# Attention, dense layers and top-2 experts in one kernel: the attention's opening by head, its transfers in a written order, and fillers while rows are gathered

## The chip, the cores and the metric

The kernel runs on one core of a Trainium2 chip. The core has TensorE (PE in the rows: matmuls, and PEld for its weight loads), VectorE (DVE), ScalarE (ACT), GpSimd (POOL) and SyncE (SP, which here only issues transfers). The engines run on their own and wait for each other by semaphores. The metric is the time of one execution on the device in microseconds (us); smaller is better. The profile is one execution, taken by the hardware profiler.

## What is computed

Three layers in a row, all in float32: attention with rotary positions over 2 batches x 8 heads x 576 places x 64 dimensions; a dense layer 512 -> 2048 -> 512 with a leaky maximum on 1152 tokens; and a layer of 8 experts (512 -> 1024 -> 512), of which each token takes the two with the highest noisy score.

```python
q_rot, k_rot = (rotate(q), rotate(k))              # x1*cos - x2*sin | x1*sin + x2*cos
scores = scale * np.matmul(q_rot, k_rot.transpose(0, 1, 3, 2))
scores = scores - np.max(scores, axis=-1, keepdims=True)
attn = np.exp(scores)
attn = attn / (np.sum(attn, axis=-1, keepdims=True) + 1e-09)
x = np.matmul(attn, v)                             # then to tokens x 512
h = x @ w_in
x = np.maximum(0.01 * h, h) @ w_out
# experts: the two highest of x @ w_gate + log1p(exp(x @ w_noise)) * noise, then
h = np.maximum(x[mask] @ w1[e], 0.0)
out[mask] += top2_w[mask, k, None] * (h @ w2[e])
```

## The kernel before

Numbers are kept to nearly float32 by splitting an operand into a high part (what PE's fast float32 form keeps) and a low part (the rest), and adding products of both.

**Attention** goes over eight pairs of heads. For a pair: q and k are loaded (`load_qk`), rotated by four elementwise operations for each of the two (`rope`: times cos, two halves times sin, the sum), and turned on PE (`turn`, L329 for one head of pair 0, L331 for both heads at once). ScalarE copies the high part out of PSUM (`turn_high`, L340), VectorE makes the low part (`turn_low`, L356), and small transfers on the chip copy high parts to other partitions (`turn_copy`, TQ<-TQ and TK<-TK; for the first k ScalarE does it, L346). A first set of products gives only each row's maximum (`max_scores` on PE, L377; `max_reduce` on VectorE, L384; five or nine tiles). The maxima are turned to a row (`max_turn`, L394 and L398) and put beside q by ScalarE (head 0 of pair 0, L403) or by a transfer (`max_put`, TQ<-mr), so that the second set of products (`scores`, L427) comes out less its maximum. ScalarE takes the exponential (L433), PE multiplies by v (`values`, L446, which also sums the rows), and the sums go by four small transfers, a reciprocal on VectorE and a product on GpSimd into x.

The order of all this is written out by hand: the string `ORDER` has a letter for each step (M, D: product and maximum; S, W: scores and exponential; V: values; O, P: a rotation on VectorE, on GpSimd; Q, K: turning q, k; a, b, e: the copies; l: loading q, k; F and the signs ! # $ % & *: loading and converting the first six weight tiles of the dense layer; o: a filler, `busy`, a matmul on zeros that keeps PE at work). Every engine but SP runs its steps in the order of the letters. On SP the order of the transfers was left to a scheduler. Three PSUM buffers (the digit behind a letter) take M, S, Q, K and R in turn, one takes V.

In the opening, pair 0 is loaded with both heads in one transfer, and its eight rotations of head 0 stand on VectorE, those of head 1 on GpSimd, both as soon as the data are there. All later rotations are GpSimd's. The conversion of the first weight tiles (L199 to L212) starts in pair 0.

**Dense layer** (L586, L595): 16 slices of weights, converted as it goes. **Experts**: the routing is worked out, an expert's rows are gathered from memory by GpSimd's indirect transfers (`gather`, L890: three of at most 128 rows), turned on PE (`turn_x`, L730) and multiplied (L586, L999). Fillers stand on PE before and between these.

Of the kernel before, what the change touches and what calls it, by code (L numbers as in the profile page):

```python
# [82 lines left out]
def fused_kernel(ctx, tc, q, k, v, w_in, w_out, w_gate, w_noise, noise, w1, w2, consts, out):  # L83
# [149 lines left out]
    ET = mybir.EngineType  # L233
    order = ExitStack()
    order.enter_context(tc.manual_schedule(engines={ET.PE, ET.Activation, ET.DVE, ET.Pool}))
    raw, TQ, TK, VF, VT = [], [], [], [], []
    for i in range(NSET):
        if i < 2:
# [63 lines left out]
    def rope(pr, n, eng, i, a0=0, a1=2):  # L302
        x = raw[pr % 2][n]
        if (pr, n) not in roped:
            roped[pr, n] = [a2.tile([128, KT, 2, D], F32, name=m) for m in ("rope_" + n, "rope_t")]
        hs = slice(a0, a1)
        r, t = (y[:, :, hs] for y in roped[pr, n])
        rv, tv = (y.rearrange("p j h d -> p h j d") for y in (r, t))
        if i == 0:
            eng.tensor_tensor(rv, x[:, hs], cosb[:, hs], op=OP.mult)  # L310
        elif i < 3:
            o, z = (0, 32) if i == 1 else (32, 0)
            eng.tensor_tensor(tv[..., o:o + 32], x[:, hs, :, z:z + 32], sinb[:, hs, :, o:o + 32], op=OP.mult)
# [193 lines left out]
    ORDER = (
"cucluyuluyulxffyflfxzywzxwIzxwzvwvOPvOlvOPlvOPwOoooooooooooooooooQ0POwOhPQ1wOjK2aPhPwijPabnlPooooK0lM1iM2lDPbn"
"oM1lPDM0lPDM2lZDoM1ZPDZM0ZDZM2ZPDM1ZlPDM0lDPR2FDFQ1mFS2PhlR0hjamjPWeK0eS2PiaS1inPVbWnbWVlP!lS2!#lS0$PWM1VWPDM2"
"!M0PDM1VDS2PlDM0Wl%S1M2PD&FVWDPR0US1*PM2mtV#WDePS0l$M1WS2lVDPW%Q0P!#FM1hK2PDVhajiaR1PjVbmineS1&PeS0nWVb*PWl$M2"  # L510
"PUwS1M0wWVDtP!DM1tS2DwVWPw%M0lS1#PTlDPVsW$lM2FS0%lVDWl#R1BM0$mS2BVeWDM1U%S2M0DWtVDNS2VWXQ1M0YhK2DVhajPiaR0jVbm"
"ineS0PeS1nWPbVWPM2wUS0DM1wWVDPtM2tS0DwVPWwPM1lS2TDsPVlWM0lS1DlVWBBR2M0mS1DeVWM2US0DM1WtVNDS2VXWYQ0M1hK2DPVhaji"
"aR1jVbmPineS1PeS0nWbVPWM2wUS1DPM0wWVDtM2tPS1DwVPWwM0PS2TDsVWM1S0DVBWBR2M1mS0DeVWM2US1DM0WNtVDS2VXWYQ1M0hK2DPVh"
"ajiaR0jVPbmineS0PeS1nWPbVWM2wUS0PDM1wWVDtM2PtS0DwVPWwPM1S2TDsVWM0S1DVBWBR2M0mS1DeVWM2US0DM1WNtVDS2VXWYQ0M1hK2D"
"VhajiaR1jVbmineS1eS0nWbVWM2wUS1DM0wWVDtM2tS1DwVWwM0S2TDsVWM1S0DVBWBR2M1mS0DeVWM2US1DM0WtNVDS2VXWQ1YM0hK2DVhaji"
"aR0jVbmineS0&eS1nWbV*WM2wUS0DM1wWVDt&M2tS0&*wVWDw!M1*S0TDsVW#$M2S1DVWB%R0BM2mS1D&eVW*M0US2DM1WtVDNS0VWXM2S1DVY"
"WR0VmeS2eVWS1US0WtVtWVS2TVsWS1VWS0BVWBS2US1WtVWVNVVXVYUtt")
# [637 lines left out]
```

## Time and profile before

| | |
|---|---|
| time, median of 3 runs | 671.38 us (670.01 to 676.26) |
| the profiled execution's own time, and its span | 673.01 us, 670.9 us |
| PE busy | 639.8 us (95% of the span) |
| DVE, ACT, POOL busy | 398.3, 317.0, 170.3 us |
| granted PE clock, mean over the span | 0.990 of full |
| attention, PE's first filler to its last product by v | 1.3 to 182 us |
| dense layer | 182 to about 396 us |
| routing and first gather | about 396 to 412 us |
| experts | 412 us to the end |

A row of a timeline has the start in us from the span's beginning, the time from the first to the last instruction of the row, engine, line, operation, out<-in, shapes, and how many; in brackets the time in which the engine stood idle before it, and what it waited for. Matmuls overlap each other, so the pace of PE is read from the distance of two starts. The granted clock 1.00 is 2.4 GHz, 0.50 is 1.2 GHz.

### The profile page before, as it was taken

The page shows a single profiled execution, that of the slowest core. Times are in us where ns is not written, and L with a number is a line of the kernel's source. Part 1 is how long each engine was busy: PE and PEld are TensorE (multiplying, and loading weights), DVE is VectorE, ACT ScalarE, POOL GpSimd, SP SyncE. Part 2 cuts the span into 40 slices and gives each one's busy share as a digit, 9 for nine tenths or more (in the row PEclk, how much of TensorE's full clock was granted, in tenths as well). Part 3 has the DMA queues.
Part 4 walks back from the last instruction along what each step waited for, and adds up shares of the span by engine and source line. Part 5 has one row for each costly group of instructions (what it writes and reads, how often), then busy time and mean ns, then how long its engine had stood idle before and what let it go on. Part 6 is the DMA issues. An engine that isn't in the chain of part 4 may idle for free. (4 is left out here: it accounts for less than half of the span.)

```text
span 670.9 us, 10384 instructions
## 1 busy us (share of the span) xinstructions
PE 639.8 (95%) x3655; PEld 551.3 (82%) x3659; DVE 398.3 (59%) x830; ACT 317.0 (47%) x643; POOL 170.3 (25%) x179
## 2 busy tenths in 40 slices
PE   7698999999999999999999998999999999999993
PEld 3487788888878888889799975888888888888882
DVE  8788555556069988863237664565665656575611
ACT  4454556665444644432235441545454545454511
POOL 9973777111111000000000001132305050504102
PEclk9999999999999999999999998999999999999998
DMA  6657433325039443310164442557667575848423
GB/s 175 196 159 225 117 74 81 73 67 198 27 111 331 149 129 126 126 48 0 63 236 126 126 112 54 166 132 198 151 210 170 160 205 158 204 147 203 103 28 41
DMA packets 88958, 90.70 MB, mean 135 GB/s; under 512 B 21443, under 2 KB 66694, under 8 KB 88902
## 3 DMA queue, kind: packets, MB, share of 16 engines
q1 hardware_dynamic: 84006, 79.11, 40.0%
q0 software_dynamic: 4608, 10.49, 7.8%
q8 instruction: 30, 0.49, 0.3%
q10 hardware_dynamic: 288, 0.39, 0.2%
q14 instruction: 26, 0.21, 0.1%
HBM read 69.95 MB, written 14.19 MB: 125 GB/s over the span
## 5 line engine op out<-in xcount | busy, mean ns | idle before, releaser
L218 DVE TENSOR_TENSOR wl<-raw,wh 128x512 fp32r<-128x512 f32 x108 | 72.5, 688 | 49.7 <-ACT wh L216 48.4
L1016 POOL DMA_INDIRECT out<-y_row,idx x24 | 41.2, 1718 | 177.0 <-ACT y_row L1008 172.6
L216 ACT ACTIVATE wh<-raw 128x512 fp32r<-128x512 f32 x108 | 66.5, 629 | 34.1 <-DMA raw<-in_moe_w 33.4
L384 DVE TENSOR_REDUCE maxes<-pM 128x1 fp32r<-128x576 f32 (+1 forms) x73 | 54.2, 754 | 43.2 <-PE pM L377 42.5
L890 POOL DMA_INDIRECT got<-x_rows,idx x24 | 23.6, 985 | 216.5 <-DVE gate L842 199.8
L999 PE MATMUL bank<-wh,g_x 128*128 128x512 f32 x216 | 78.4, 403 | 0.1
L446 PE MATMUL pO<-p,VF 128*128 128x288 f32 x256 | 72.7, 413 | 0.0
L433 ACT ACTIVATE p<-pS 128x576 f32<-128x576 f32 (+1 forms) x73 | 46.4, 649 | 53.2 <-PE pS L427 51.6
L586 PE MATMUL bank<-xe_h,wh 128*128 128x320 f32 x216 | 67.8, 314 | 0.0
L586 PE MATMUL bank<-xe_h,wl 128*128 128x320 f32 x216 | 67.7, 313 | 0.0
L586 PE MATMUL bank<-xe_l,wh 128*128 128x320 f32 x216 | 66.5, 310 | 0.0
L607 ACT ACTIVATE g_t<-bank 128x512 f32<-128x512 f32 (+2 forms) x48 | 23.4, 488 | 85.3 <-PE bank L586 85.3
L608 DVE TENSOR_TENSOR g_f<-bank,g_t 128x512 f32<-128x512 f32 (+2 forms) x48 | 26.7, 555 | 51.8 <-ACT g_t L607 51.6
L446 PEld LDWEIGHTS pO<-p,VF 128*128 128x128 f32 x256 | 45.3, 192 | 8.9 <-issue 1.1
L595 PE MATMUL bank<-g_h,wh 128*128 128x384 f32 (+2 forms) x152 | 51.9, 341 | 0.0
L586 PE MATMUL bank<-xh,wh 128*128 128x384 f32 (+2 forms) x152 | 51.5, 339 | 0.0
L586 PE MATMUL bank<-xl,wh 128*128 128x384 f32 (+2 forms) x152 | 51.3, 338 | 0.1
L586 PE MATMUL bank<-xh,wl 128*128 128x384 f32 (+2 forms) x152 | 51.4, 338 | 0.0
L595 PE MATMUL bank<-g_l,wh 128*128 128x384 f32 (+2 forms) x152 | 51.2, 337 | 0.0
L595 PE MATMUL bank<-g_h,wl 128*128 128x384 f32 (+2 forms) x152 | 51.0, 336 | 0.0
L982 DVE SCALAR_TENSOR_TENSOR g_x<-bank,g_x 128x320 fp32r<-128x320 f32 x64 | 31.0, 484 | 29.5 <-ACT g_x L981 29.5
L999 PEld LDWEIGHTS bank<-wh,g_x 128*128 128x128 f32 x216 | 40.4, 188 | 8.1 <-DVE g_x L982 0.8
(238 smaller groups left out, 1488.0 us busy)
## 6 DMA issues: line engine op xcount, KB each, us to landing
raw<-in_moe_w SPq DMA_DIRECT2D x128, 256.0 KB, 2.9
raw<-in_moe_w_in SPq DMA_DIRECT2D x16, 512.0 KB, 3.9
raw<-in_moe_w_out SPq DMA_DIRECT2D x16, 512.0 KB, 3.9
inv_sum<-inv_sums SPq DMA_DIRECT2D x16, 144.0 KB, 3.2
out<-none SPq DMA_DIRECT2D x9, 256.0 KB, 6.8
raw_q<-in_q SPq DMA_DIRECT2D x8, 256.0 KB, 2.8
raw_k<-in_k SPq DMA_DIRECT2D x8, 256.0 KB, 3.6
VF<-in_v SPq DMA_DIRECT2D x16, 128.0 KB, 2.6
```

The costliest lines, as they stand in the source:

```text
L216: A.activation(hi[:, part], t, AF.Copy)
L218: V.tensor_tensor(lo[:, part], t, f32(hi)[:, part], op=OP.subtract)
L384: V.tensor_reduce(maxes[pr % 2][rows, i:i + 1], maxed.pop((pr, a, j))[rows, :, 0:288], axis=AX.XY, op=OP.max, negate=True)
L433: A.activation(t[r], scored.pop((pr, a, j))[r, :, 0:288], AF.Exp, scale=0.125)
L446: T.matmul(acc[g][:, z, 0:288], w, p[r, z, :], start=opens, stop=closes)
L586: T.matmul(h[:, :n], w[:, 0, k * 128:(k + 1) * 128], m[:, k, cols:cols + n], start=(i == 0), stop=(i == 11))
L595: T.matmul(b[:, o:o + n], w[:, 1, ds], m[:, :n], start=(first and opens and t == 0), stop=(last and t == 2), skip_group_check=True)
L608: V.tensor_tensor(g[:, :n], h[:, :n], t[:, :n], op=OP.max)
L890: G.indirect_dma_start(out=t[:n], out_offset=None, in_=x1_rows, in_offset=bass.IndirectOffsetOnAxis(ap=idx[e][:n, st:st + 1], axis=0))
L982: V.scalar_tensor_tensor(g[:, C:2 * C], h[:, :C], 0.0, f32(g)[:, :C], op0=OP.max, op1=OP.subtract)
L999: T.matmul(yr[st], s, w, start=(f == 0 and t == 0), stop=(f == 7 and t == 2))
L1016: s = G.indirect_dma_start(out=out, out_offset=bass.IndirectOffsetOnAxis(ap=idx[e][:n, st:st + 1], axis=0), in_=r[:n], in_offset=None, com ...
```

## The change

1. `load_qk` can load one head and take another queue. Pair 0's head 0 is loaded by SP (letter l), its head 1 by ScalarE's queue (letter k).
2. A copy of one element on GpSimd (`after_first`, letter p) reads the last result of VectorE's rotation of k. GpSimd's rotation of head 1 stands behind it.
3. The rotation of pair 1's k is VectorE's (`ROPE_V`).
4. SP's transfers, too, keep the order of the letters all through attention (`tc.manual_schedule(engines={ET.SP})`).
5. `ORDER` is new. Pair 0's second head has its maxima among the first head's scores and values; the small loads (Z) and the loads and conversions of the dense layer's six weight tiles stand in pairs 3 to 7; 27 fillers in place of 23.
6. In the routing 12 fillers in place of 3 behind the first table, and 4 and 2 behind the first two turned tiles of gathered rows.
7. The matmul for the fifth maxima tile of a `DIRECT` head reads 64 partitions in place of 128.

```diff
+    att.enter_context(tc.manual_schedule(engines={ET.SP}))
...
-    def load_qk(pr, n, part):
+    def load_qk(pr, n, part, a=slice(0, 2), queue=None):
...
+        heads = [S * D, a.stop - a.start]
         if part == 0:
-            nc.sync.dma_start(t[:, :, 0:4, :].rearrange("p h j d -> p h (j d)"),
-                              bass.AP(tensor=src.tensor, offset=base, ap=[[4 * D, 128], [S * D, 2], [1, 4 * D]]))
...
+            (queue or nc.sync).dma_start(t[:, a, 0:4, :].rearrange("p h j d -> p h (j d)"),
+                                         bass.AP(tensor=src.tensor, offset=base, ap=[[4 * D, 128], heads, [1, 4 * D]]))
...
+    def after_first():
+
+        G.tensor_copy(pause, roped[0, "k"][0][0:1, 0, 0, 0:1])
...
-            T.matmul(p[:1, 512:576], m[:, 4:5], ident_r[:, 64 * a:64 * a + 64], start=True, stop=True)
+            r = slice(64 * a, 64 * a + 64)
+            T.matmul(p[:1, 512:576], m[r, 4:5], ident_r[r, r], start=True, stop=True)
...
-    DIRECT = ((0, 0),)
+    DIRECT, ROPE_V = ((0, 0),), ((1, 'k'),)
     ORDER = (
-"cucluyuluyulxffyflfxzywzxwIzxwzvwvOPvOlvOPlvOPwOoooooooooooooooooQ0POwOhPQ1wOjK2aPhPwijPabnlPooooK0lM1iM2lDPbn"
...
+"cucluyuluyulxffyflfxzykzxkzIxzkzkvwOvvOwvOwvOOoooooooooooooooooQ0wOlOhOlpPjooK1aPliPlbnPwooooM2M0wPDQ1lDPM2hlPD"
...
+    halves = [[(0, n, i, slice(a, a + 1), x) for n in "qk" for i in range(2)] for a, x in enumerate((nc.sync, nc.scalar))]
...
-            "l": (load_qk, [(pr, n, i) for pr, n in pairs for i in range(2)]),
+            "l": (load_qk, halves[0] + [(pr, n, i) for pr, n in pairs[2:] for i in range(2)]),
+            "k": (load_qk, halves[1]),
...
-    busy(bank[3], 3)
+    busy(bank[3], 12)
     r1[8](1)
     onehot(1, range(T1, NJ))
     for st in range(3):
         turn_x(0, st, bank[(0, 1, 5)[st]])
-        busy(bank[3], (0, 0, 3)[st])
+        busy(bank[3], (4, 2, 3)[st])
```

The rows below are instructions in the order in which they stand, without times; the changed kernel's line numbers are 9 to 13 higher.

PE before, from the maxima of pair 0's first head: pR turns maxima, pT turns q or k (of pair 1 here), pS are scores, pO values, pM products for the maxima.

```order
L394 MATMUL pR<-ident_r,maxes_119 1x128 x4
L395 MATMUL pR<-ident_r,maxes_119 1x64
L331 MATMUL pT<-ct,rope_q 128x128 x5
L427 MATMUL pS<-TQ_111,TK_112 128x288 x4
L398 MATMUL pR<-ident_r,maxes_119 5x128
L331 MATMUL pT<-ct,rope_k 128x128 x5
L427 MATMUL pS<-TQ_111,TK_112 128x288 x8
L446 MATMUL pO<-p,VF_117 128x288 x4
```

PE of the change, from pair 0's first scores:

```order
L437 MATMUL pS<-TQ_113,TK_114 128x288 x16
L456 MATMUL pO<-p,VF_119 128x288 x2
L386 MATMUL pM<-TK_114,TQ_113 128x288 x6
L456 MATMUL pO<-p,VF_119 128x288 x2
L386 MATMUL pM<-TK_114,TQ_113 128x288 x2
L456 MATMUL pO<-p,VF_119 128x288 x2
L386 MATMUL pM<-TK_114,TQ_113 128x288 x2
L340 MATMUL pT<-ct,rope_q 128x128 x5
L340 MATMUL pT<-ct,rope_k 128x128 x5
L408 MATMUL pR<-ident_r,maxes_121 5x128
```

Before, all maxima of pair 0 stood ahead of its first scores; now four tiles of scores come first, and the second head's five tiles of maxima stand between values, ahead of pair 1's turning.

VectorE before, behind its rotations:

```order
L356 TENSOR_TENSOR TQ_111<-pT,TQ_111 64x576 x2
L356 TENSOR_TENSOR TK_112<-pT,TK_112 64x576
L384 TENSOR_REDUCE maxes_119<-pM 128x1
L356 TENSOR_TENSOR TK_112<-pT,TK_112 64x576
L384 TENSOR_REDUCE maxes_119<-pM 128x1 x3
L384 TENSOR_REDUCE maxes_119<-pM 64x1 x2
L384 TENSOR_REDUCE maxes_119<-pM 128x1 x4
L356 TENSOR_TENSOR TQ_113<-pT,TQ_113 64x576 x2
L356 TENSOR_TENSOR TK_114<-pT,TK_114 64x576 x2
L203 TENSOR_SCALAR word<-word 128x512
L205 TENSOR_SCALAR word<-word 128x512
```

VectorE of the change:

```order
L365 TENSOR_TENSOR TK_114<-pT,TK_114 64x576
L393 TENSOR_REDUCE maxes_121<-pM 128x1 x3
L365 TENSOR_TENSOR TQ_113<-pT,TQ_113 64x576
L393 TENSOR_REDUCE maxes_121<-pM 128x1
L393 TENSOR_REDUCE maxes_121<-pM 64x1
L365 TENSOR_TENSOR TK_114<-pT,TK_114 64x576
L313 TENSOR_TENSOR rope_k<-raw_k_123,ct_att 128x2x5x64
L316 TENSOR_TENSOR rope_t<-raw_k_123,ct_att 128x2x5x32 x2
L318 TENSOR_TENSOR rope_k<-rope_k,rope_t 128x640
L393 TENSOR_REDUCE maxes_121<-pM 64x1
L393 TENSOR_REDUCE maxes_121<-pM 128x1 x4
```

The four rotations of pair 1's k now stand between the maxima of pair 0's first head and those of its second; the weight conversion (L203, L205) is gone from here.

SP before, where pair 1's copies stand (raw without a letter is a weight tile):

```order
L173 DMA raw<-in_moe_w_in 128x4x256
L176 DMA raw<-in_moe_w_out 128x1024
L173 DMA raw<-in_moe_w_in 128x4x256
L280 DMA raw_k_121<-in_k 128x2x256
L350 DMA TQ_113<-TQ_113 64x576
L414 DMA TQ_111<-mr 1x4x128
L416 DMA TQ_111<-mr 1x16x4
L350 DMA TQ_113<-TQ_113 64x576
L348 DMA TK_114<-TK_114 64x576 x2
```

SP of the change:

```order
L283 DMA raw_k_123<-in_k 128x2x256
L286 DMA raw_k_123<-in_k 64x2x64
L359 DMA TQ_115<-TQ_115 64x576
L283 DMA raw_q_117<-in_q 128x2x256
L424 DMA TQ_113<-mr 1x4x128
L426 DMA TQ_113<-mr 1x16x4
L359 DMA TQ_115<-TQ_115 64x576
L357 DMA TK_116<-TK_116 64x576 x2
```

The three weight loads ahead of the copies are gone. One load of pair 4's q (raw_q_117, into the buffer that GpSimd's rotation of pair 2's q reads) stands ahead of the maxima of pair 0's second head (TQ<-mr).

## Rows read from the trace of the kernel before

**Rows 1.** Timeline of PE in pair 0: start, us, what, idle before.

```profile
11.23 0.74 PE L329 MATMUL pT<-ct,rope_k 128*64 128x128 f32 x5 [1.78 <-DVE rope_k L315]
...
13.36 0.53 PE L377 MATMUL pM<-TK,TQ 128*128 128x288 f32 x2
...
20.62 0.40 PE L394 MATMUL pR<-ident_r,maxes 128*1 128x128 f32 x4
...
21.87 0.77 PE L427 MATMUL pS<-TQ,TK 128*128 128x288 f32 x4
...
32.80 0.50 PE L377 MATMUL pM<-TK,TQ 128*128 128x288 f32 x2 [3.80 <-DMA TK<-TK]
```

**Rows 2.** Timeline of PE without gaps, pairs 2 to 6, and the dense layer's first matmul.

```profile
93.51 0.69 PE L427 MATMUL pS<-TQ,TK 128*128 128x288 f32 x4
94.05 0.43 PE L377 MATMUL pM<-TK,TQ 128*128 128x288 f32 x2
94.31 1.17 PE L446 MATMUL pO<-p,VF 128*128 128x288 f32 x4
95.10 0.63 PE L377 MATMUL pM<-TK,TQ 128*128 128x288 f32 x2
...
108.96 0.44 PE L398 MATMUL pR<-ident_r,maxes 128*5 128x128 f32 x1
...
128.00 0.44 PE L398 MATMUL pR<-ident_r,maxes 128*5 128x128 f32 x1
...
182.08 0.61 PE L586 MATMUL bank<-xh,wh 128*128 128x512 f32 x1
```

**Rows 3.** DMA issues from 20 to 34 us, then one row of the whole span.

```profile
raw<-in_moe_w_in SPq DMA_DIRECT2D x2, 512.0 KB, 6.0
...
TK<-TK SPq DMA_DIRECT2D x2, 144.0 KB, 5.0
...
TK<-TK SPq DMA_DIRECT2D x11, 144.0 KB, 2.5
```

**Rows 4.** Engines in windows of 1 us: busy times, granted clock, DMA share, GB/s.

```profile
34.00:35.00 1.00, 1.00 (x4) 0.70 (x3) 0.10 (x1) 0.00 (x0) 0.92 (x3) 0.50 0.82 171
...
413.00:414.00 1.00, 1.00 (x5) 1.00 (x4) 0.00 (x0) 0.00 (x0) 0.00 (x0) 0.50 0.07 16
```

**Rows 5.** Timeline of DVE in the opening: rotations, then maxima.

```profile
5.23 0.49 DVE L310 TENSOR_TENSOR rope_q<-raw_q,ct_att 128x320 f32<-128x320 f32 x1
...
7.84 1.15 DVE L310 TENSOR_TENSOR rope_k<-raw_k,ct_att 128x320 f32<-128x320 f32 x1
...
15.58 6.32 DVE L384 TENSOR_REDUCE maxes<-pM 128x1 fp32r<-128x576 f32 x9
```

**Rows 6.** Timeline of POOL: first rotation, then two of whole pairs.

```profile
5.28 1.17 POOL L310 TENSOR_TENSOR rope_q<-raw_q,ct_att 128x320 f32<-128x320 f32 x1 [0.44 <-DMA raw_q<-in_q]
...
11.87 1.53 POOL L310 TENSOR_TENSOR rope_q<-raw_q,ct_att 128x640 f32<-128x640 f32 x1
...
16.65 1.55 POOL L310 TENSOR_TENSOR rope_k<-raw_k,ct_att 128x640 f32<-128x640 f32 x1
```

**Rows 7.** Timeline of ACT's queue and of ACT in the opening.

```profile
1.27 0.50 ACTq L525 DMA_DIRECT2D ct<-in_constants  x1
...
5.66 0.30 ACT L256 COPY VT<-zero 64x128 f32<-64x128 f32 x1
```

**Rows 8.** Timeline of PE round the first gather.

```profile
403.58 2.75 PE L140 MATMUL bank<-warm 128*128 128x512 bf16 x12
...
409.04 0.66 PE L730 MATMUL bank<-ct,got 128*128 128x128 f32 x4 [1.96 <-DMA got<-x_rows,idx]
410.53 0.66 PE L730 MATMUL bank<-ct,got 128*128 128x128 f32 x4 [0.83 <-DMA got<-x_rows,idx]
...
413.22 0.47 PE L586 MATMUL bank<-xe_h,wl 128*128 128x320 f32 x1
413.49 0.47 PE L586 MATMUL bank<-xe_h,wh 128*128 128x320 f32 x1
```

More of the change, by code (lines that the diff above doesn't have):

```diff
@@ L277, in load_qk @@
         src, t = q if n == "q" else k, raw[pr % 2][n]
-        base = src.offset + (b * H + h0) * S * D
+        base = src.offset + (b * H + h0 + a.start) * S * D
+        heads = [S * D, a.stop - a.start]
         if part == 0:
-            nc.sync.dma_start(t[:, :, 0:4, :].rearrange("p h j d -> p h (j d)"),
-                              bass.AP(tensor=src.tensor, offset=base, ap=[[4 * D, 128], [S * D, 2], [1, 4 * D]]))
-        else:
-            nc.sync.dma_start(t[0:64, :, 4, :],
-                              bass.AP(tensor=src.tensor, offset=base + 512 * D, ap=[[D, 64], [S * D, 2], [1, D]]))
+            (queue or nc.sync).dma_start(t[:, a, 0:4, :].rearrange("p h j d -> p h (j d)"),
+                                         bass.AP(tensor=src.tensor, offset=base, ap=[[4 * D, 128], heads, [1, 4 * D]]))
+        else:
+            (queue or nc.sync).dma_start(t[0:64, a, 4, :],
+                                         bass.AP(tensor=src.tensor, offset=base + 512 * D, ap=[[D, 64], heads, [1, D]]))
     def load_v(pr, part):
@@ L315, in rope @@
             eng.tensor_tensor(r, r, t, op=OP.add)
+    pause = ap.tile([1, 1], F32, name="pause")
+    def after_first():
+        G.tensor_copy(pause, roped[0, "k"][0][0:1, 0, 0, 0:1])
     def ps(n, name, shape=(128, 2, 512), dt=F32):
@@ L505, in fused_kernel @@
     FILL_T, FILL_V = 'ADP', 'PA'
-    DIRECT = ((0, 0),)
+    DIRECT, ROPE_V = ((0, 0),), ((1, 'k'),)
     ORDER = (
-"cucluyuluyulxffyflfxzywzxwIzxwzvwvOPvOlvOPlvOPwOoooooooooooooooooQ0POwOhPQ1wOjK2aPhPwijPabnlPooooK0lM1iM2lDPbn"
[L509 to L517, printed above, removed]
+"cucluyuluyulxffyflfxzykzxkzIxkzkvwOvvOwvOwvOOoooooooooooooooooQ0wOlOhOlpPjooK1aPliPlbnPwooooM2M0wPDQ1lDPM2hlPD"
+"M0aPjM2wPlDK1lDiPwnooR0bPmOooS2OS1WOS0OWS2PWVWM1M0DPM2lVlDM1lVDPlDPM0Q2DPK1hR0VhajPmljiS0einQ2ePWnahVPbhjbPS0U"
+"ljS1aWS2PlWS0lVWtWPM1aM2DM0PVDPM1VDDM2PlM0lDM1VDPR2DM0PmeM2DK1PDS0iibnR2PmlnWS2eVWPebS0PUlM1S2PWDtVWtwM0PM1DS2"
+"wVwTWDPsM0M2wDPS1lDPlVWBR0BM2mS1lDM0WeVDlM2S1DVNWM0US2DQ1XtR0PVWmK2heYS0hejVaijaiPVnbWPS1nbVPWS0VWPllM2US1DwM0"
+"PWVtDPtM2S1wDPM0wWVDwM2TlS1DslR0WVmM2eS1DBM0WVDBM2S1DVWM0US2NDQ1WtR0VZhPXajK2mZVhYeijS0eiVanPWbnS1PbVWZPZS0ZVW"
+"PM2wUS1DM0ZWVPtDtPM2S1ZDM0wPWVTwDM2sS1wDR0WVBmBM2S1eDM0WVDM2S1DNVWM0US2DQ1XtR0PVWmK2heYS0hejVaijaiPVnbWPS1nbVP"
+"WS0VWPM2wUS1DM0PwWVDtPM2tS1DPwM0WVwDM2TsS1DR0WVBmM2BS1DeM0WVDM2S1DVNWM0US2DQ1XtR0VWYFmK2heS0hjeViajaiVnbWS1nbV"
+"FWFS0VWS2wUM1M0wWDVt!DM2tS1DwM0WVwDM2#$S1VDW%R0M2mS1FD&M0eVWD!M2TS1*sVDW#M0US1$Q2WtVDBhB%K1haR0j&VamjieS0*ieS2"
+"VbnNWbWnVF!S0X#V$WM2wUS1%M0wDYWVt&DM1tS2DwM0WVwD!FM1*S2TDsV#W$R0M1mS2DeM0WVDBM1%S2BDV&W*M0S1UDS2WtR0NVWmV!eeX#"
+"S1$VWYVS2V!%WS0#US1$S2WttW%VWVT&s&*V*S0BVWBS1VWS2US0NWtVWVXVYVVUtt")
     pairs = [(pr, n) for pr in range(NP) for n in "qk"]
@@ L526, in fused_kernel @@
                   [(0,), (1,)]),
-            "l": (load_qk, [(pr, n, i) for pr, n in pairs for i in range(2)]),
+            "l": (load_qk, halves[0] + [(pr, n, i) for pr, n in pairs[2:] for i in range(2)]),
+            "k": (load_qk, halves[1]),
             "f": (fill_raw, [(i, n) for i in range(2) for n in "qk"]),
             "I": (lambda: V.tensor_copy(ident_r, ident), [()]),
-            "O": (rope, first[0]),
-            "P": (rope, first[1] + [(pr, n, G, i) for pr, n in pairs[2:] for i in range(4)]),
+            "p": (after_first, [()]),
+            "O": (rope, first[0] + [(pr, n, V, i) for pr, n in pairs[2:] if (pr, n) in ROPE_V for i in range(4)]),
+            "P": (rope, first[1] + [(pr, n, G, i) for pr, n in pairs[2:] if (pr, n) not in ROPE_V for i in range(4)]),
             "Q": (turn, [(0, "q", 0), (0, "q", 1)] + [(pr, "q", None) for pr in range(1, NP)]),
```

## Prediction

> **What bounds the kernel now.** I read the page's engine lines first: PE is busy for 95% of the span, so a gain can only come out of PE's remaining waits, or of work that PE did slowly. Then the timeline of PE, stage by stage. From the middle of attention on it has no gaps, and one pair takes 19.04 us from turning its maxima to the next pair's [rows 2]. The dense layer and the experts look the same, and the change doesn't touch them. So two places matter: attention up to about 75 us, and the first gather.
>
> How much is lost in attention? PE's first scores start at 21.87, the dense layer's first matmul at 182.08 [rows 1, 2]: 160.2 us. What PE does in between is eight pairs at 19.04, that is 152.3, less what pair 0 has had by then: eleven groups for maxima at 0.26, about 2.9, and two turned tensors, a turned row and pair 1's turned q, together about 1.9 (0.55 for a tensor, 0.26 for a row, my estimates from starts in that timeline). 152.3 - 4.8 = 147.5, so 12.7 us of that stretch are **waste**. The reader sees most of it in one row: PE waits 3.80 us at 29.0 for the copy TK<-TK [rows 1]. The list of issues says why: that copy took 5.0 us to land where the same copy takes 2.5 in the median, and ahead of it on the queue are weight loads of 512 KB with 6.0 us each [rows 3]. Behind the wait PE runs at half clock: the granted clock is 0.50, the 1.2 GHz level, at 34 us [rows 4], and stays low for about 3.4 us, which loses about 1.7. The remaining 7.2 us are shorter waits up to 72 us, each for a copy or for VectorE, whose conversions stand between maxima.
>
> Ahead of that, the opening is one chain: VectorE's rotations, the turned k, its copies, the maxima, the scores. VectorE's eight rotations run from 5.23 to 11.2, where PE turns k [rows 1, 5], while GpSimd rotates the other head. The first takes 0.49 and has almost started alone (GpSimd's starts at 5.28); the same operation on k takes 1.15 with GpSimd at work [rows 5, 6].
>
> **The change, part by part.**
>
> *VectorE first.* The constants land as before, so the first rotation starts at 5.23. Alone, a rotation of 320 columns takes 0.49 [rows 5] with about 0.41 to the next start; the two of 160 columns are between 0.25 and 0.41 each, I take 0.25. Four are 1.3 us, eight are 2.6: k is rotated at 7.85, where it was 11.2. From the turning of k to the first product for maxima it was 13.36 - 11.23 = 2.13 [rows 1], so 10.0 now. ScalarE, which makes both copies in that chain, was done with its fills at 5.96 and now also issues four loads at 0.50 each [rows 7], which puts it at 8.0; its three copies of 0.65 then end at 9.95. I take 10.2 (bounds 9.9 and 10.8). The bytes of head 0 are half of what was loaded first, so I count no delay there.
>
> *Maxima and scores.* A maximum costs 0.70 (nine in 6.32 [rows 5]). The first starts 0.65 behind its product, at 10.85; the five of head 0 and one low part between them (0.77) end at 15.1. From there to the scores it was 21.87 - 20.62 = 1.25 [rows 1], so **scores start at 16.4, 5.4 us earlier**. PE then still owes the five maxima groups of head 1 (5 x 0.26 = 1.3) and pair 1's turned q (0.55), which before were done: the net is **3.5 us**.
>
> *GpSimd later.* It starts head 1 at 7.9. With its pace beside VectorE (8 operations from 5.28 to 11.9) it ends at 14.5, where it ended at 11.9. Head 1's k must be turned and copied by about 19 us, when PE reaches its maxima: 14.5 and some 4 us of turning, copying and landing. That is hidden, with about 0.5 us to spare; without it PE would lose what it is late.
>
> *Pair 1's k on VectorE.* Four operations of 640 columns, behind the last low part of pair 0 at 15.9. Alone they would take twice 1.3, that is 2.6. GpSimd is at work without a pause (1.53 for an operation, 4.78 for a tensor [rows 6]); beside GpSimd k took 11.2 - 7.84 = 3.4 for half the columns [rows 1, 5], so twice that, 6.8, is the other bound. The row beside GpSimd is the nearest, and the first operation may find GpSimd between two of its own, so I take 6.2, to 22.1. Head 1's five maxima are queued behind it and end at 25.6. PE meanwhile has four tiles of scores, three of values, five maxima groups and two turned tensors: 4 x 0.53 + 3 x 0.97 + 1.3 + 1.1 = 7.4 (values are 0.79 and 0.18 more that the next group waits [rows 2]), which would end at 23.8. So **PE waits about 2.0** here (0 if alone, 2.5 at most by the rows).
>
> The Trainium skill has a rule on this (page SBUF — State Buffer, section Who interferes with whom): a VectorE instruction with two inputs in SBUF and a GpSimd instruction that reads SBUF exclude each other for the whole instruction, while one with a single SBUF input runs beside GpSimd. The trace agrees: 0.49 against 1.15 for the rotation, and GpSimd keeps 1.53 to 1.55 while VectorE reduces maxima out of PSUM [rows 5, 6]. By that rule the sum would be 1.2 us worse; the case stands among the rivals.
>
> *SP's written order.* Head 1's maxima (TQ<-mr) now stand behind the load of pair 4's q, which can be issued only when GpSimd has rotated pair 2's q: two tensors behind 14.5, at 4.8 each and some 1.5 of exclusion, 25.6. Then load, two puts of about 0.7 and 2.3 to land: 29.8. PE wants them at 25.7 plus one tile of values, one of scores, a turned q and values (3.2): 28.9. I count a wait of **1.0** (0 to 2). The copies TK<-TK of pair 1 come next, about 2.0 later, and PE wants them 3 us later: hidden, now that they land in 2.5 and no weight load is ahead [rows 3].
>
> *Late conversion.* What it removes from the opening is the 3.80 wait, the half clock behind it and VectorE's conversions between maxima. Where it goes VectorE is busy for about half of the time, and PE's values of the last pairs need no VectorE, which covers it; without that cover each of the four moved tiles would cost 2.9 us on VectorE.
>
> *Sum of attention.* Waste after the first scores: 12.7 before; after 2.0 + 1.0 + 2.0 of small waits = 5.0. The last is my choice: the pairs without gaps [rows 2] speak for 0, the 7.2 us of shorter waits before for up to half of that, 3.6. Gain 3.5 + 7.7 = **11.2**.
>
> *The gather.* PE's three fillers end at 407.1, it waits 1.96 for rows until 409.04 and 0.83 for the next ones [rows 8], and then the granted clock is 0.50 at 413 [rows 4], with 0.27 between matmul starts [rows 8]. Eleven or twelve such matmuls at the half clock are 3.3 us; at full clock half of it, **1.5 less**. Twelve fillers at 0.216 (2.59 for twelve, 403.58 to 406.17 [rows 8]) end at 409.1 in place of 407.1, four are 0.86 in a wait that was 0.83, two are 0.43 in a shorter one: together **0.2 more** (0 to 0.5). Bounds: 1.5 gained, or, if the clock falls all the same and all fifteen are on the path, 3.2 lost. The rows speak for the first: PE waited 1.96 and then fell to half clock, and behind the full 12 fillers of 403.58 it had been at full clock.
>
> *The sum:* 11.2 + 1.3 = 12.5 us. The profiled execution's 673.0 becomes 660.5. Its time is 1.6 above the median of the runs shown, 671.4, so I give **658.9** for the median.
>
> **The rivals.** *Written queue, late copies:* SP waits in line, and a load that waits for GpSimd holds a copy on which PE waits, in pairs 1 to 3. For it: GpSimd starts 2.6 later and pair 4's load stands ahead of TQ<-mr. Against: from pair 2 on, GpSimd is almost a pair ahead. Its price is the wait of before with its half clock again, 3.8 + 1.7 = 5.5: 664.4. *The wait moves with the weights:* the loads of 512 KB now stand among the copies of pairs 4 to 6. If four copies wait 2.5 more each [rows 3], 10 us go: 668.9, no change. Against: in the second half of attention before, PE had no such wait although weights were loaded there. *Slower:* in every pair from 1 to 7 one copy is issued behind a transfer that itself waits for a landing. Each costs an issue of 0.6 and 2.5 to land, 3.1; seven are 21.7: 680.6. From 1.8 us a pair on the change is slower than before. Against it: in the order of the letters, the transfers that wait for sums stand behind the maxima's puts. *Fillers on the path:* 12.5 - 4.5 = 8.0 gained: 663.4. *VectorE and GpSimd take strict turns on pair 1's k:* 2.6 + 4.8 = 7.4 in place of 6.2, 660.1; this lies inside the main case. *The change of the opening does less:* VectorE is not faster alone (0.49 was chance): k at 11.2, 3.3 of the gain gone, 662.2.
>
> **How the numbers follow.** Main case 0.58 (0.2 of it with strict turns), its own range 655.5 to 662. Late copies 0.17, weights 0.10, slower 0.05, fillers 0.05, opening 0.05. With no wait but the small ones it would be 655.9; with the worst bound of each term (1.2 more in the rotations, 1 in the puts, 0.6 in the opening, 1.6 in small waits, but not the gather's 4.5) 663.3. I give 655 to 667, which holds the main case, late copies and the small ones, and leaves out the weights' case and the slower one. A measurement here can tell about 1%, 6.7 us, from no change. Under 664.7 are the main case, half and more of late copies, fillers and opening: 0.78. Within 1%: 0.17. Slower by over 1%: 0.05.
>
> **What would show it.** Right: VectorE's first eight rotations last under 3 us; PE's first L377 (now L386) at about 10.2 and first scores at about 16.4; no wait of PE near 4 us for TK<-TK; rotations of pair 1's k of 6 us, with PE waiting some 2 us near 24; the dense layer's first matmul near 171; granted clock 1.00 at 413, and about 1.3 us less there. Wrong: a queue row of SP that waits for GpSimd with a copy behind it and PE idle for that copy; PE idle in the pairs where weights are loaded; a clock of 0.50 in the opening, where PE has about 70% of work.

## The result

The changed kernel takes 666.90 us (median of 11; 664.35 to 668.71), the kernel before 671.85 in the same comparison (670.01 to 677.16). The ratio is 0.991, with a 95% interval of 0.9883 to 0.9937: 5.0 us gained by the medians and 6.0 by the ratio (4.2 to 7.9 by its interval). That is clear of no change, but under the 1% from which the prediction counted a change as faster. The forecast of 658.9 is missed by 8.0 us. The time lies at the upper end of the range, and what was expected as a gain of 12.5 is less than half of that.

| | before | after |
|---|---|---|
| the profiled execution's own time, and its span | 673.01, 670.9 | 665.30, 663.4 |
| first product for maxima | 13.36 | 9.96 |
| first scores | 21.87 | 15.40 |
| dense layer's first matmul | 182.08 | 176.99 |
| behind the twelve fillers of the gather, from their start to the first product by second weights | 14.30 | 12.72 |
| mean granted clock | 0.990 | 0.995 |

The two profiled executions stand 7.5 us apart in their spans, more than the medians do: that of before is 1.2 over its median, that of after 1.6 under. The 7.5 us are 5.1 in attention, 1.6 in the gather and 0.9 in the experts (the sum is rounded). The change doesn't touch the experts, so the 0.9 is spread; the dense layer took the same.

PE after, the rows that answer to [rows 1] and [rows 2]: start, us, what, idle before in brackets.

```profile
7.86 0.71 PE L338 MATMUL pT<-ct,rope_k 128*64 128x128 f32 x5
9.96 0.79 PE L386 MATMUL pM<-TK,TQ 128*128 128x288 f32 x4 [0.53 <-ACT TK L355]
15.40 0.94 PE L437 MATMUL pS<-TQ,TK 128*128 128x288 f32 x3
23.00 0.53 PE L386 MATMUL pM<-TK,TQ 128*128 128x288 f32 x2 [2.19 <-DVE maxes L393]
28.38 0.74 PE L340 MATMUL pT<-ct,rope_q 128*128 128x128 f32 x5 [0.64 <-DVE TQ L365]
32.17 1.30 PE L437 MATMUL pS<-TQ,TK 128*128 128x288 f32 x8 [0.64 <-DVE set_q L365]
43.07 0.80 PE L437 MATMUL pS<-TQ,TK 128*128 128x288 f32 x4 [0.92 <-ACT mr L416]
60.89 0.74 PE L340 MATMUL pT<-ct,rope_k 128*128 128x128 f32 x5 [2.54 <-ACT mr L416]
...
99.93 0.30 PE L340 MATMUL pT<-ct,rope_k 128*128 128x128 f32 x1 [0.87 <-ACT mr L416]
...
176.99 0.61 PE L599 MATMUL bank<-xh,wh 128*128 128x512 f32 x1
```

The wait of 3.80 us for TK<-TK is gone, and no wait for a copy is left. The half clock behind it is gone too: windows of 4 us of before, then of after, with the granted clock behind POOL's busy time.

```profile
33.00:37.00 4.00, 4.00 (x14) 3.33 (x14) 2.07 (x3) 0.00 (x0) 3.92 (x5) 0.57 0.73 195
```

```profile
33.00:37.00 4.00, 4.00 (x22) 3.08 (x21) 1.86 (x3) 1.19 (x2) 4.00 (x4) 1.00 0.68 187
```

But others stand in its place, the longest 2.54 and 2.19. By the prediction's own account (from the first scores to the dense layer, less 147.5 us of work; after, 1.9 more, since that much is still owed) the **waste** was 160.2 - 147.5 = 12.7 before and is 161.6 - 149.4 = 12.2 now. It should have been 5.0.

### The profile page after: what moved, and what is told of

It reads as the page before. It is cut to its first block, busy times and chain, and to the rows that moved or that the text cites. A ratio compares the mean times of both kernels' runs of the same rounds, so it can differ in the third digit from the quotient of the medians.

```text
span 663.4 us, 10431 instructions
## 1 busy us (share of the span) xinstructions
PE 639.3 (96%) x3674; PEld 550.6 (83%) x3678; DVE 398.3 (60%) x834; ACT 315.7 (48%) x643; POOL 165.8 (25%) x176
```

## The experiments

All are set against the kernel before: x_later, b_first, pool_k1 and sp_free on one chip, the others on a second, which is also that of after_again, the changed kernel unaltered. The medians of before there were 674.4 to 675.2, so ratios are compared and not times. Waste is worked out as above, from one traced execution of each run.

| run | first scores | dense layer | waste | ratio (95%) |
|---|---|---|---|---|
| after_again (no edit) | 15.45 | 176.40 | 11.6 | 0.9884 (0.9850 to 0.9919) |
| x_later | 15.55 | 174.90 | 10.0 | 0.9841 (0.9817 to 0.9864) |
| b_first | 16.11 | 175.42 | 9.9 | 0.9874 (0.9850 to 0.9898) |
| both | 15.23 | 174.05 | 9.4 | 0.9850 (0.9813 to 0.9888) |
| p2 | 15.08 | 175.57 | 11.1 | 0.9849 (0.9814 to 0.9885) |
| both_p2 | 16.07 | 172.79 | 7.3 | 0.9815 (0.9780 to 0.9849) |
| pool_k1 | 15.17 | 179.91 | 15.3 | 0.9880 (0.9857 to 0.9903) |
| no_p | 17.06 | 179.94 | 13.5 | 0.9926 (0.9899 to 0.9954) |
| sp_free | 15.91 | 186.24 | 20.9 | 0.9996 (0.9976 to 1.0015) |
| graft | 15.17 | 178.72 | 14.2 | 0.9934 (0.9907 to 0.9961) |
| graft_free | 15.85 | 182.95 | 17.7 | 0.9995 (0.9971 to 1.0019) |
| b_late (old opening) | 22.57 | 176.61 | 6.5 | 0.9883 (0.9831 to 0.9934) |
| b_late_sp (old opening) | 22.65 | 189.34 | 19.2 | 1.0052 (1.0017 to 1.0087) |
| b_gather (old opening) | 23.23 | 184.04 | 13.3 | 0.9979 (0.9951 to 1.0006) |

> The changed kernel unaltered, on the chip on which the three kernels behind it run, so that they can be set against it. It should give a ratio to the kernel before of 0.988 to 0.994.

It does, with 0.9884. Its trace shows how far one execution can differ from the next: two waits of PE for a row of maxima (mr) are 0.56 and 1.44 us, where that of after has 2.54 at 60.89 and 0.87 at 99.93.

```profile
59.77 0.74 PE L340 MATMUL pT<-ct,rope_k 128*128 128x128 f32 x5 [0.56 <-ACT mr L416]
...
99.37 0.74 PE L340 MATMUL pT<-ct,rope_k 128*128 128x128 f32 x5 [1.44 <-ACT mr L416]
```

### The wait at 61 us: step X and inv_sum

ScalarE and GpSimd after, round PE's wait of 2.54, and SP ahead of it.

```profile
53.73 1.19 SPq L490 DMA_DIRECT2D inv_sum<-inv_sums  x2
```

```profile
58.09 1.40 POOL L494 TENSOR_TENSOR inv_sum<-unnorm,inv_sum 128x576 f32<-128x576 f32 x1 [9.71 <-DMA inv_sum<-inv_sums]
```

```profile
59.52 0.69 ACT L506 ACTIVATE xh<-inv_sum 128x576 fp32r<-128x576 f32 x1 [2.81 <-POOL inv_sum L494]
60.11 0.63 ACT L443 ACTIVATE p<-pS 128x576 f32<-128x576 f32 x1
60.65 0.25 ACT L416 ACTIVATE mr<-pR 5x128 fp32r<-5x128 f32 x1
```

Read from below: PE waits for the row of maxima (mr); it stands on ScalarE behind an exponential and behind the high part of x (xh, letter X), and ScalarE stood still for 2.81 us for GpSimd's product, which waited for the two transfers of inv_sum.

The pattern isn't new. In the kernel before X stood ahead of a row of maxima too, with three copies between, and in one pair PE waited 1.41 us behind it:

```profile
68.76 0.69 ACT L496 ACTIVATE xh<-inv_sum 128x576 fp32r<-128x576 f32 x1 [2.29 <-POOL inv_sum L484]
...
71.52 1.56 PE L427 MATMUL pS<-set_q,set_k 128*128 128x288 f32 x8 [1.41 <-ACT mr L406]
```

The change moved the row of maxima up, so that only one exponential is left between it and X.

x_later moves X behind the copies, in four pairs (in one of them Y, GpSimd's low part of x, moves along). This and the edits below show a piece of the order's string:

```diff
-...US2DQ1XtR0PVWmK2heY...
+...US2DQ1tR0PVWmK2heXY...
```

> The changed kernel with step X of four pairs (ScalarE's copy of the high part of x, which waits for GpSimd's product) put behind the pair's row of maxima and the copies of its turned tensors; nothing else differs. Theory (the new order puts X ahead of the row of maxima, and PE waits behind it): the waits of PE of 2.54 us at 60.9 and 0.87 at 99.9 of the changed kernel's trace vanish, the dense layer starts about 3.4 earlier than 176.99, and the time against the kernel before falls from 0.991 to about 0.987. Rival (inv_sum lands late, and whatever stands next waits for it in its place, or the slack is eaten by VectorE or SP): the gaps move by less than 2 us and the time stays at 0.990 to 0.992.

```profile
57.51 0.27 ACT L416 ACTIVATE mr<-pR 5x128 fp32r<-5x128 f32 x1
57.68 0.62 ACT L349 ACTIVATE TQ<-pT 64x576 fp32r<-64x576 f32 x1
59.17 0.69 ACT L506 ACTIVATE xh<-inv_sum 128x576 fp32r<-128x576 f32 x1 [0.87 <-POOL inv_sum L494]
```

The row of maxima is made at 57.51 in place of 60.65 and both waits of PE are gone; a new one of 0.72 at 62.23 gives some back. The dense layer starts 2.1 earlier than in after, and 1.5 earlier than in after_again, where 3.4 were expected.

b_first leaves X and moves SP's loads behind the transfers of inv_sum (B):

```diff
-...sM0M2wDPS1lDPlVWBR0BM2m...
+...sM0M2wDPS1DPVWBR0BllM2m...
```

> The changed kernel with SP's loads of raw q and k in two pairs put behind the two transfers that bring the reciprocal sums back (inv_sum), which stood behind them in the written queue; nothing else differs. Theory (SP's written order makes inv_sum late): the transfers of inv_sum, issued at 53.73 in the changed kernel's trace, are issued about 2.0 us earlier, GpSimd's product starts at about 56 in place of 58.1, and PE's wait of 2.54 at 60.9 falls to about 0.5; some 2 us gained. Rival (the transfers' own landing of over 4 us sets it, or the loads that move make a later rotation late): the wait stays over 1.5, no gain or a loss.

inv_sum was issued at 52.53 in place of 53.73, less than the 2.0 expected, and PE's wait at 61 was gone all the same; that at 98.25 (1.00), in a pair that the edit doesn't touch, stayed. But after_again, with no edit, issued inv_sum at 52.62 and had only 0.56 of that wait. So x_later shows that X stood in the wrong place; that SP's line makes it late is what the trace of after shows (a load, raw_q, took SP 1.41 us right ahead of inv_sum, 0.63 in after_again), and b_first doesn't separate its gain from the spread of one execution to the next. Put together:

> The changed kernel with both small repairs together: step X behind the copies of the pair's turned tensors, and SP's loads of raw q and k of two pairs behind the transfers of inv_sum. Alone they took the dense layer's start from 176.99 to 174.9 and 175.4. Theory (both attack the same wait at 60.9, and each takes one of the two smaller ones): PE's waits at about 61, 98 and 62 are all under 0.5, 3.5 to 4 us of attention gained against the changed kernel, ratio lower than the changed kernel's by 0.005. Rival (X moved far enough makes b's order indifferent): the same as with X alone.

Neither wait is left, and waste fell to 9.4 us; the ratio doesn't separate this from X alone.

### VectorE beside GpSimd

p2 holds GpSimd, by a second copy of one element, while VectorE rotates pair 1's k:

```diff
-        G.tensor_copy(pause, roped[0, "k"][0][0:1, 0, 0, 0:1])
+        G.tensor_copy(pause, roped[pr, "k"][0][0:1, 0, 0, 0:1])
...
-...OooS2OS1WOS0OWS2P...
+...OooS2OS1WOS0OpWS2P...
```

> The changed kernel with a second one-element copy on GpSimd, which reads VectorE's rotated k of pair 1 and stands ahead of GpSimd's last step on pair 1's q: GpSimd stands still while VectorE rotates pair 1's k; nothing else differs. Theory (the rotation takes 6.2 us and not 2.6 because GpSimd is at work beside it): it takes 2.6 to 4, the maxima behind it start 2 to 3.5 earlier, PE's wait of 2.19 at 20.8 to 23.0 falls under 0.5, and the shorter waits behind it (0.64, 0.64, 0.92) shrink; 2 to 4 us gained against the changed kernel, since GpSimd's next results are needed 8 us later. Rival (VectorE's rotation is slow by itself at this size, or by the products beside it): it still takes 5 us or more and nothing is gained. Second rival: GpSimd, held by 2 to 4 us, is late later (PE waits for a turned q or k of pair 2), no gain.

VectorE's four rotations after, then in p2.

```profile
15.92 1.31 DVE L313 TENSOR_TENSOR rope_k<-raw_k,ct_att 128x640 f32<-128x640 f32 x1
17.15 3.61 DVE L316 TENSOR_TENSOR rope_t<-raw_k,ct_att 128x320 f32<-128x320 f32 x2
20.79 1.36 DVE L318 TENSOR_TENSOR rope_k<-rope_k,rope_t 128x640 f32<-128x640 f32 x1
```

```profile
15.60 1.50 DVE L313 TENSOR_TENSOR rope_k<-raw_k,ct_att 128x640 f32<-128x640 f32 x1
17.02 0.88 DVE L316 TENSOR_TENSOR rope_t<-raw_k,ct_att 128x320 f32<-128x320 f32 x2
17.93 0.82 DVE L318 TENSOR_TENSOR rope_k<-rope_k,rope_t 128x640 f32<-128x640 f32 x1
```

6.2 us became 3.2, of which the first step still met GpSimd. PE's wait of 2.19 is gone, and it turns pair 1's q at 25.60 in place of 28.38. Of these 2.8 only 1.1 is left in the waste: at 57.49 PE waits 1.94 and at 98.89 1.57, both again for the row of maxima behind X, and behind the first of them it ran at half clock:

```profile
58.00:60.00 2.00, 2.00 (x10) 1.59 (x8) 1.25 (x2) 1.93 (x4) 2.00 (x3) 0.65 0.01 1
60.00:62.00 2.00, 2.00 (x6) 1.42 (x5) 1.77 (x3) 0.69 (x2) 1.92 (x2) 0.50 0.92 215
```

The mean granted clock was 0.991 in this execution and 0.993 or 0.994 in the other four, so part of this loss is that of the traced one. With the waits behind X repaired as well the gain holds:

> The changed kernel with all three repairs: step X behind the copies of the turned tensors, raw loads behind the transfers of inv_sum, and GpSimd held while VectorE rotates pair 1's k. Theory (they are separate places of one sum): the waits of PE at 23 and 57 to 61 and 99 are all under 0.6 us, the waste behind the first scores is 6.5 to 7.5 us in place of 12.4, the dense layer starts at 170.5 to 172 (the prediction's 171), the time against the kernel before is 0.979 to 0.982. Rival (what is gained early is given back, as in the run with GpSimd held alone, where the wait at 57.5 grew to 1.94): dense start at 173 to 174.5, ratio 0.984 or more.

```profile
26.61 0.74 PE L340 MATMUL pT<-ct,rope_q 128*128 128x128 f32 x5 [0.64 <-DVE TQ L365]
...
172.79 0.61 PE L599 MATMUL bank<-xh,wh 128*128 128x512 f32 x1
```

Waste is 7.3, no wait of PE in attention is over 0.91 us, and the time is 663.19 against 675.23: 12.0 us less. It is the lowest ratio of all, just clear of that of after_again on the same chip, but its interval overlaps those of x_later, both and p2. The rival's waits (57.5, 99) didn't come back, and of the 2.8 us of both and the 1.1 of p2 nothing is lost: waste is 4.9 under that of after. The theory's numbers were a little too good (dense layer at 172.8 with first scores 0.7 later than after, where 170.5 to 172 was expected), and the upper end of the ratio's interval, 0.9849, reaches into the rival's range.

pool_k1 gives pair 1's k back to GpSimd:

```diff
-    DIRECT, ROPE_V = ((0, 0),), ((1, 'k'),)
+    DIRECT, ROPE_V = ((0, 0),), ()
```

> The changed kernel with the rotation of pair 1's k on GpSimd again; its four steps stand at the same places of the order, and VectorE has only pair 0's first head. Theory (VectorE's rotation costs 6.2 us between maxima and makes PE wait 2.19 at 20.8): that wait goes, but GpSimd, which ends pair 1's q first, brings k 5 us later, so PE waits 2 to 4 us for pair 1's turned k at about 30 to 35; the time is 0 to 2 us longer than that of the changed kernel. Rival (GpSimd has time enough): the wait of 2.19 goes and nothing comes in its place, 2 us faster.

The wait of 2.19 went, and one of 2.37 came at 27.68, behind GpSimd. This one profiled execution then ran at half clock.

```profile
24.00:28.00 4.00, 1.63 (x11) 1.14 (x10) 3.02 (x4) 2.09 (x4) 3.92 (x5) 1.00 0.38 93
28.00:32.00 4.00, 4.00 (x15) 2.78 (x13) 1.51 (x2) 2.04 (x3) 3.92 (x4) 0.54 0.57 137
32.00:36.00 4.00, 4.00 (x16) 3.31 (x15) 0.00 (x0) 2.60 (x4) 3.92 (x5) 0.61 0.60 140
```

With 671.27 us it was also the slowest of six (the others 665.59 to 668.73), so its waste of 15.3 speaks for that execution alone. By the ratio, whether VectorE or GpSimd rotates pair 1's k makes no difference that can be measured.

no_p takes away the copy that holds GpSimd in the opening (the letter p leaves the order).

> The changed kernel without the one-element copy that holds GpSimd until VectorE has rotated head 0's k; nothing else differs. Theory (the two engines hinder each other in rotations, 0.49 against 1.15 us): k is rotated at about 10 to 11 in place of 7.6, the first product for maxima comes 2.5 to 3.3 us later than 9.96, GpSimd ends pair 0's second head about 2.5 us earlier, and PE's wait of 2.19 at 20.8 shrinks or stays; the time is 1.5 to 3 us longer than that of the changed kernel. Rival (0.49 was chance, the loads by head make the opening): first product within 0.7 us of 9.96 and the same time.

PE turns k at 9.50 in place of 7.86 and the first product for maxima stands at 11.62 in place of 9.96: 1.7 us, less than the 2.5 to 3.3 expected, and the first scores 1.7 later. The time between the ratios (0.9926 against 0.991 and 0.9884) is of the size expected, but their intervals overlap, and part of it may be the clock: the trace has a wait of 2.43 at 62.24 with a granted clock of 0.63 and 0.51 from 62 to 66 behind it, and ten of the eleven executions have a mean of 0.989 to 0.992, where those of after have 0.991 to 0.995.

### Late weights and SP's order

sp_free leaves SP's order to the scheduler:

```diff
-    att.enter_context(tc.manual_schedule(engines={ET.SP}))
```

> The changed kernel without the written order on SP: a scheduler places SP's transfers, as in the kernel before; nothing else differs. Theory (the written queue is worth little, what is lost sits in the order of ScalarE and VectorE): within 2 us of the changed kernel, with PE's waits at 20.8 and 60.9 still there. Rival (the written queue carries the gain of the attention): the copies TK<-TK of the first pairs land late again, PE waits 2 us or more for one of them, and the time goes 3 us or more towards the kernel before. Second rival (the written queue costs): 2 us or more faster than the changed kernel, with inv_sum issued earlier.

SP, then PE, of this run.

```profile
40.59 0.38 SPq L173 DMA_DIRECT2D raw<-in_moe_w_in  x1
41.04 0.49 SPq L176 DMA_DIRECT2D raw<-in_moe_w_out  x1
41.58 1.48 SPq L173 DMA_DIRECT2D raw<-in_moe_w_in  x1
43.16 0.83 SPq L421 DMA_DIRECT2D TQ<-mr  x1
```

```profile
49.67 0.82 PE L436 MATMUL pS<-TQ,TK 65*128 65x288 f32 x2 [6.04 <-DMA TQ<-mr]
```

Without the written order the whole gain is gone (0.9996). In the changed kernel the first weight load is issued at 118.07; here the scheduler issues three loads of 512 KB from 40.6 on, whatever the place of their letters, and they stand ahead of the maxima's put, for which PE then waits.

So I expected late letters alone to bring little. b_late moves F and the conversions in the kernel before, and nothing else:

```diff
-...lPDM0lDPR2FDFQ1mFS2PhlR0hjamj...lS2!#lS0$PWM1V...
+...lPDM0lDPR2DQ1mS2PhlR0hjamj...lS2lS0PWM1V...
```

> The kernel before with the loads and conversions of the dense layer's six weight tiles moved in the written order to where the change has them (each behind the same product by v, pairs 4 to 7); SP's order is still a scheduler's. Theory (a scheduler issues a weight load as soon as its buffer is free, so the letter's place says little, as the run with a free SP showed at 40.6 us): a copy or a put of the first pairs still lands late behind 512 KB loads, the waits of PE in pairs 0 to 2 sum to 4 us or more, and 0 to 3 us are gained. Rival (the place in the order is enough): the wait of 3.80 us for TK<-TK and the half clock behind it go, 5.5 us or more gained, ratio 0.992 or less.

```profile
26.72 1.87 SPq L348 DMA_DIRECT2D TK<-TK  x2
...
30.71 0.60 SPq L173 DMA_DIRECT2D raw<-in_moe_w_in  x1
...
32.55 0.59 SPq L176 DMA_DIRECT2D raw<-in_moe_w_out  x1
...
33.86 0.62 SPq L173 DMA_DIRECT2D raw<-in_moe_w_in  x1
```

My theory was wrong and the rival right: waste fell from 12.7 to 6.5 and the ratio, 0.9883, is that of the whole change. The scheduler does issue the loads early, but with these letters they fall behind pair 1's copies, where before they stood ahead of them, and PE waits no more than 0.75 us until 137 (2.29 for TK<-TK at 144.82 is the longest behind it). The half clock at 34 is gone, but this execution has one of its own at 20 to 24 (0.57), and its six executions have mean clocks from 0.979 to 0.993; the ratio's interval is wide. Late weights under a written SP:

> As the run before this one (late weights in the kernel before) with SP's transfers, too, in the written order through attention. Theory (late weights need SP's written order to be late): the wait of 3.80 for TK<-TK is gone or under 1 us, granted clock 1.00 through the first 60 us, 4 to 6 us gained against the kernel before and 2 us or more against the kernel with late weights alone. Rival (the letters of the kernel before were not written for SP, so that its copies now stand behind loads that wait for GpSimd): waits of 2 us and more in several pairs, no gain or slower.

The rival again: with the old letters SP's line has loads among the copies of pairs 5 and 6, PE waits 3.41 at 129.83 and 3.08 at 154.77 for TK<-TK, and the kernel is slower than before, by 0.5%. Not all of the 19.2 us of waste is the letters': from 20 to 32 us the mean clock of this execution was 0.57. This is the rival of the prediction in which the wait moves with the weights.

graft takes the change's opening and, from pair 1's first maxima, the old letters with late weights; two groups of loads stand behind their pair's copies.

> The changed kernel up to its first tile of maxima of pair 1; from there the written order of the kernel before, with the weights' loads and conversions late as in the run with late weights (two groups of loads put behind the copies of their pair), and SP in the written order. Theory (the opening and the late weights are worth what the prediction said, and the new order of the later pairs costs the rest): PE's waste behind pair 0 is under 4.5 us where the changed kernel has about 7, the dense layer starts 2 to 4 us earlier than the changed kernel's, ratio lower by 0.003 to 0.006. Rival (late weights fit only with the new order): waits of 2 to 4 us in pairs 5 and 6, as in the run of the kernel before with late weights and a written SP, and no gain against the changed kernel or a loss.

graft_free is the same without SP's written order:

> The changed kernel's order up to its first tile of maxima of pair 1, from there the letters of the kernel before with late weights, and SP's order left to the scheduler as before. Theory (the scheduler of SP does well with the old letters and late weights, which had 6.7 us of waste): waste 8 to 10 us, of which 5 in pair 0 as in the changed kernel, dense start 172 to 174, ratio 0.982 to 0.986. Rival (a free SP puts weight loads ahead of a put or a copy here too, as in the changed kernel with a free SP): a wait of 3 us or more in pairs 0 to 2, dense start at 177 or later, ratio 0.99 or more.

Both fail, graft_free in the way of its rival. graft has none of the waits of 2 to 4 us that its rival named; it has small ones in many places (the longest behind pair 0 is 1.11 at 86.14) and more waste than the change, and why stays open. In graft_free a load stands ahead of the put once more, as in sp_free, and PE waits 4.26 at 47.95. Neither way of putting the old letters behind the new opening kept their 6.5 us of waste.

### The gather alone

```diff
-    busy(bank[3], 3)
+    busy(bank[3], 12)
...
-        busy(bank[3], (0, 0, 3)[st])
+        busy(bank[3], (4, 2, 3)[st])
```

> The kernel before with the change's fillers round the first gather alone (12 behind the first table in place of 3; 4 and 2 behind the first two turned tiles). Theory (prediction: the clock does not fall, 1.5 less, the fillers 0.2 more): granted clock 1.00 at the first products of gathered rows, 1.3 us between the first gathered tile on PE and the first products by the second weights less than before, ratio 0.998. Rival (all fifteen are on the path): 3 us longer, ratio 1.004.

The rows of this kernel that answer to [rows 8]:

```profile
405.62 2.75 PE L140 MATMUL bank<-warm 128*128 128x512 bf16 x12
408.51 2.75 PE L140 MATMUL bank<-warm 128*128 128x512 bf16 x11
411.10 0.63 PE L730 MATMUL bank<-ct,got 128*128 128x128 f32 x4
...
418.52 0.47 PE L999 MATMUL bank<-wh,g_x 128*128 128x512 f32 x1
```

From the twelve fillers to the first product by second weights it is 12.90, where it was 14.30 (403.58 to 417.88): 1.4 us gained, as expected. The time, 0.9979, agrees but can't be told from no change.

## Why the prediction was right or wrong

**The opening: right, and a little small.** k is rotated at 7.6 (7.85 predicted), the first product stands at 9.96 (10.2), the first scores at 15.40 (16.4). Net of the 1.9 us owed that is 4.6 in place of 3.5. Two errors met here, which is luck: VectorE's eight rotations took 3.0 us and not 2.6, and they began at 4.60, 0.6 earlier than the 5.23 that was carried over from before. no_p shows what part GpSimd's pause has in it: 1.7.

**GpSimd later, hidden: right.** It ends head 1 at 13.4 (14.5), and PE's products for that head don't wait for it.

**Pair 1's k: right in size.** 6.2 us and a wait of 2.19 (6.2 and 2.0). p2 shows the cause. That VectorE and GpSimd exclude each other is the rule of the Trainium skill (page SBUF — State Buffer, section Who interferes with whom) that the prediction weighed (what it took from there on a single input leaves out that the page excepts the 2-port modes; no sum rests on it). Here GpSimd's own operations grew too, its sum of 640 columns from 1.53 (in p2) to 2.02, but 6.2 is less than the 7.4 of strict turns: the measurement decides.

**SP's written order: wrong in kind.** The 1.0 us for TQ<-mr didn't come. What SP's line held up, in the trace of after, was inv_sum at 53.73; in after_again it left 1.1 earlier. The rival of late copies by a written queue came near the mechanism (a load holds up the transfer behind it) but named the copies as what is held. And a cost was all I saw in it, where sp_free shows that without it the new letters gain nothing.

**The late conversion: right where it was taken away, too cheap where it went.** The wait of 3.80 and the half clock behind it are gone, and by itself it takes 6.2 us of waste away (12.7 to 6.5 in b_late). But it was put at nothing in the later pairs, because VectorE was busy there for half of the time. With the conversions VectorE is busy for about 80%, and the pair with most of them takes PE 20.19 us, from one row of maxima to the next pair's, where the same work took 19.05 before: 1.1 us (1.7 in both_p2, 126.71 to 147.46, where two short waits of PE, 0.47 and 0.18, are for VectorE's maxima). PE after, then before; below them VectorE's busy time (the third) in two windows after and one before.

```profile
131.45 0.41 PE L408 MATMUL pR<-ident_r,maxes 128*5 128x128 f32 x1
...
151.64 0.22 PE L408 MATMUL pR<-ident_r,maxes 128*5 128x128 f32 x1
```

```profile
139.24 0.44 PE L398 MATMUL pR<-ident_r,maxes 128*5 128x128 f32 x1
...
158.29 0.44 PE L398 MATMUL pR<-ident_r,maxes 128*5 128x128 f32 x1
```

```profile
120.00:140.00 20.00, 20.00 (x118) 17.33 (x116) 15.83 (x25) 13.09 (x23) 0.00 (x0) 1.00 0.54 167
140.00:160.00 20.00, 19.75 (x109) 16.39 (x108) 16.61 (x24) 12.26 (x23) 4.97 (x4) 1.00 0.71 221
```

```profile
100.00:120.00 20.00, 20.00 (x120) 17.51 (x119) 10.81 (x15) 11.17 (x19) 12.30 (x10) 1.00 0.33 80
```

**The small waits: this step failed.** I put them at 2.0 us and took 3.6 as their bound, since the pairs of before ran without gaps [rows 2]. But that was a property of the old letters, and the change writes the order of every pair anew. The shorter waits of before weren't all "for a copy or for VectorE" either: 1.20 at 23.90 and 1.41 at 71.52 were for a row of maxima that ScalarE makes, the second behind X, and this was the chain to look for in the new order. Measured, 12.2 - 2.2 for pair 1's k leaves 10.0. Step X and its inv_sum hold 2.2 to 2.8 of that by x_later, b_first and both (the unaltered kernel's second trace, with 11.6, would make it 0.6 less), and the late conversions 1.1. Of the 7.3 that both_p2 leaves, waits of 0.64, 0.63 and 0.91 (at 26.61, 30.40 and 41.28) are 2.2 and the pair with the conversions is 1.7; the remaining 3.4 is in pieces too short to follow, and stays open. (Ten groups for maxima, not eleven, stood ahead of the first scores before; that takes 0.3 from each figure of waste alike.) So attention gained 4.6 + 0.5 = 5.1, not 3.5 + 7.7 = 11.2.

**The gather: right.** 1.6 in the trace of after, 1.4 alone, 1.3 predicted; a window after, in the first products of gathered rows, has the granted clock at 1.00 where [rows 4] had 0.50:

```profile
408.00:409.00 1.00, 1.00 (x8) 1.00 (x8) 0.00 (x0) 0.00 (x0) 0.00 (x0) 1.00 0.00 0
```

So neither the range's centre nor the chance of 0.78 for faster by over 1% held: both rested on one term that I chose by the shape of the old order. both_p2, with three small moves, takes back 4.9 of the 7.2 us by which waste stood above the prediction's 5.0. Its 12.0 us against before, as much as was predicted for the change, are in part luck: its trace accounts for 9.3 in attention and 1.6 in the gather.

## What to carry to other kernels

When a change writes an order anew, the gaps of the old order don't carry over, but the chains that made them do. Go through the new order, and for each step that waits for a long chain (here X, behind GpSimd, two transfers and SP's line) look at what stands behind it on its engine. A written queue and the letters it is written for are one edit: either alone can lose all that both gain. A move that helps one place, as p2 does, may be given back at the next late step, so look for that step before counting the gain.

## What the hardware showed that I had not expected

A VectorE sum of 128x640 took 0.82 us with GpSimd held and 1.36 beside it, but two products of 128x320 went from 0.88 to 3.61: the loss isn't a fixed factor.

After a wait of 2.37 us the granted clock fell to 0.54 in the profiled execution of pool_k1, and after one of 1.94 us to 0.50 in that of p2, while after waits of 2.19 and 2.54 us it stayed at 1.00 in that of after. The length of the last wait alone doesn't tell. pool_k1's other five executions, 2.5 to 5.7 us faster, had mean clocks of 0.992 to 0.994, where the profiled one had 0.988.
